# Pooled attention into a mixture of attention experts: a written-out order of work replaced by another one

## The chip, the cores and the metric

The kernel runs on one core of one Trainium2 chip. A core has five engines with instruction queues of their own: TensorE (PE in the profile; PEld are its weight loads), VectorE (DVE), ScalarE (ACT), GpSimd (POOL) and SyncE (SP). Each engine works its queue in order and waits on semaphores for the others. Sixteen DMA engines move data; their transfers are issued here by GpSimd and SyncE. The metric is the time of one execution on the device in microseconds (us), as the median of several runs.

## What is computed

Eight batches. First an attention over pooled keys and values, then a mixture of four experts that are causal attentions themselves; the two best experts of each row are mixed by a softmax of their gate logits.

```python
k_p = k.reshape(B, H, Sp, pool, D).mean(axis=3)          # 576 rows pooled by 8 to 72; v alike
attn = softmax(scale * q @ k_p^T)                         # 8 heads, head size 64
x = (attn @ v_p) as (B, 576, 512)
logits = x @ w_gate                                       # 4 experts, the best 2 are kept
for e in range(E):                                        # each with a head size of 64
    a = softmax(causal(scale * (x @ wq[e]) @ (x @ wk[e])^T))
    out += weight[e] * (a @ (x @ wv[e]) @ wo[e])
```

## The kernel before

**Tiling.** The 576 rows of a batch are four chunks of 128 and a tail of 64; the tails of an even batch and the next odd one share a fifth chunk (index 4), which is worked with the odd batch. Heads are taken in pairs, experts in two groups g of two. PSUM is two pools: joint tiles (`jt`, two buffers) for pooling and scores, and small tiles (four buffers) for everything else. A tile comes free when it is copied out, so a step that takes a small tile waits for the copy of the fourth small tile before it, and one that takes a joint tile for the second before it. Inputs have three buffers per tensor, y has eight.

**Steps.** `plan_weights` (L844) and `plan_batch` (L869) define the work as named steps with their dependencies; nothing is issued there. A step `om3.7` is kind `om`, batch 3, number 7. The kinds, with the line that issues their instructions:

- `lh`, `ld`: half an input load, by GpSimd (L243); per batch 0,1 are k, 2,3 are q, 4,5 are v (`lh` for batch 0, issued in `first`, L807). `wi`: a weight load (L282): 0 wq, 1 wk, 2 wv, 3 the gate's, 4 wo; `wc`: its re-ordering copy on DVE (L865). `ln`, `wl`, `ql`, `xl`, `ol`, `yd` issue nothing: they only mark in the list when a transfer is taken as landed.
- `pk`, `pv`: pooling of k and v by matmuls (L290; batch 0's v in halves, L304); `kp`, `vp`: their copies; `kt`, `qm`: transposes of pooled k and of q on PE (L333, L350), `kT`, `qc`: their copies (L340, L356).
- `am`: scores of a head pair, 4 the tail columns (L370); `ae`: their exponentials on ACT (L376, L385); `om`: attention times v for a chunk and half of the heads (L396; 0 to 4 are chunks of the first half, 5 to 9 of the second); `oi`, `on`: reciprocal and normalisation on DVE (L411, L416) into x.
- `xm`, `xc`: transpose of x on PE and its copy (batches 0 to 3; L428, L436). From batch 4 on, `xd` does it by a DMA transpose on SP (L801), as `qd` does for q from batch 5 on and `od` for the experts' outputs of batches 2 to 6. The first of these transposes waits for all input and weight loads.
- `jm`, `jc`: projections to queries and keys and their copy (L461 and L471; 4 is the tail, L478 and L488); `vm`, `vc`: projections to values and logits, and copies (L441, L451, L452).
- `ga`, `gs`, `gt`, `ge`, `gb`, `gr`, `gc`: the gate's steps (DVE, POOL, DVE, ACT, POOL, DVE, POOL).
- `bm`: expert scores (L568; 0 to 4 in parts, 5 to 7 the shared tail chunk); `be`: their exponentials (L608); `bk`: causal masks on GpSimd (L623); `bo`: the experts' sums (L638; 4, in the last batch 8, is the shared tail chunk, L652 and L659); `bi`, `bg`, `bn`: reciprocal, gate factor, normalisation (L676, L680, L695).
- `ot`, `oc`: transposes of the experts' outputs on PE and copies (batches 0, 1, 7; L700, L707); `ym`, `yc`: the product with wo and its copy (L712, L723); `ys`: a store of y (L727), two DMAs for the shared chunk.
- `fo`, `fn`, `fl`, `fm`, `fc`, `fv`: a range check of all sums' reciprocals, which at the end decides whether a general version is to be run (it isn't on these inputs).
- `mz`: zeros in two buffers; `f` and `F` with a number: a filler of two matmuls on dummy data (`filler`, L766), `f` over 128 rows, `F` over 64, written into the unused end of the small tile that many places back (L775, or L779 where that tile is bf16).

**Order.** The order of the work is the string `ORDER` (L34). `emit` (L132) goes through its words and calls each step, so that the words' order is the order of each engine's queue. A last letter chooses the engine of a step that can be on several: `a` ACT, `d` DVE, `p` POOL, `s` SP. The waits are set by the data and the buffers, not by the string.

```python
    for word in ORDER.split():
        if word[0] in "fF" and word[1:].isdigit():
            filler(word[0] == "F", int(word[1:]))
            continue
        e = {"a": "ACT", "d": "DVE", "p": "POOL", "s": "SP"}.get(word[-1])
        ...
        st.fn(e)
```

Of the kernel before, what the change touches and what calls it, by code (L numbers as in the profile page):

```python
# [45 lines left out]
om1.8 bm0.4 oi1.9 wc0.3 on1.9 oi1.8 bm0.1 om1.3 kT2.0d on1.8 oi1.3 on1.3 xc1.2a be0.4 vm1.2
vm0.0 be0.1 vc1.2d vm0.3 qm2.0 vc0.3a om1.4 bm0.2 be0.2 vc0.0d oi1.4 qc2.0d on1.4 qm2.3 vm0.2
xm1.3 om0.9 bm0.0 qc2.3d am2.3 xc1.3d oi0.9 on0.9 vc0.2a be0.0 qm2.2 qc2.2d vm0.1 qm2.1 xm1.4
vm1.3 vc0.1d qc2.1d xc1.4d om1.6 ae2.3 am2.2 am2.0 ae2.2 jm1.4 ga0.0 vc1.3d oi1.6 on1.6 om1.0
om1.5 xm1.1 oi1.0 oi1.5 on1.5 on1.0 jc1.4d ae2.0 ld2.4 ld3.0 ld2.5 ld3.1 ln2.4 ln2.5 pv2.0  # L50
vp2.0a xc1.1a ld3.2 ln3.0 ln3.1 pk3.0 ln3.2 am2.1 qm3.0 vm1.4 kp3.0a vc1.4a kt3.0 kT3.0a qc3.0d
mz0.0 ld4.2 ln4.2 qm4.0 qm4.1 am2.4 jm1.1 ld4.3 bk0.2 gs0.0 bk0.0 ld3.3 bk0.4 gt0.0 qc4.0d
qc4.1d ae2.1 jm1.3 ge0.0 ae2.4 jc1.3a om2.0 xm1.0 xc1.0a jc1.1d oi2.0 on2.0 ln3.3 bm1.5 qm3.3
qm3.2 om2.2 be1.5 jm1.0 jc1.0a qc3.3d qc3.2d oi2.2 on2.2 om2.7 am3.2 ae3.2 bm1.7 be1.7 om2.6
oi2.7 oi2.6 on2.7 om2.5 oi2.5 on2.6 jm1.2 om2.1 bm1.1 jc1.2a be1.1 ld3.4 ld3.5 bk0.1 ld4.0 bk0.3
ld5.4 ld4.1 on2.5 oi2.1 on2.1 vm1.1 om2.8 qm3.1 xm2.0 oi2.8 on2.8 xc2.0d qc3.1d vc1.1a am3.3
ae3.3 ln3.4 ln3.5 pv3.0 xm2.1 xm2.2 om2.3 vp3.0a bm1.2 be1.2 am3.4 xc2.1d xc2.2d oi2.3 on2.3
# [1415 lines left out]
```

## Time and profile before

| what | value |
|---|---|
| median of three runs | 178.33 us (178.19 to 179.7) |
| the profiled execution | 178.99 us, of which 177.3 us are the span of its instructions |
| PE matmuls | 164.0 us busy, 93% of the span, 2551 recorded |
| ACT, DVE, POOL | 131.3, 122.1, 78.7 us busy |
| DMA | 30.65 MB, 173 GB/s in the mean |
| stores | 31 DMAs issued by SP, 9 by GpSimd |

How to read it: a row of a timeline has the start in us from the beginning of the span, the length, engine, line, operation, output<-inputs, and in brackets how long the engine sat idle before and what released it. PE's rows overlap: the length of a matmul's row runs to the end of its drain, and the next one starts before, so PE's pace is read from start to start. A line of the chain of waits has start, length and what the end of the span was then waiting for.

### The profile page before, as it was taken

Reading aid. Unit: us, or ns where it says so; the run is one execution under the profiler, and the core shown is the slowest. Engines: PE = TensorE matmul, PEld = TensorE weight load, DVE = VectorE, ACT = ScalarE, POOL = GpSimd, SP = SyncE. Lnnn points to the kernel's source line nnn. Section 1 sums busy time; section 2 is a strip of 40 time slices with the busy share of each in tenths; the row PEclk is TensorE's granted clock in tenths of the full one; section 3 lists DMA queues with packets and bytes.
Section 4 is the critical chain, followed back from the end, with each engine's and each line's share of the span. In section 5 each row is a group of like instructions: output and inputs, shape, how many; then the busy total and the mean of one; then the engine's idle time right before and its main releaser. Section 6 shows DMA issues by size and latency. Waiting matters only on the chain.

```text
span 177.3 us, 6308 instructions
## 1 busy us (share of the span) xinstructions
PE 164.0 (93%) x2551; PEld 131.5 (74%) x2566; DVE 122.1 (69%) x466; ACT 131.3 (74%) x239; POOL 78.7 (44%) x179
## 2 busy tenths in 40 slices
...
GB/s 23 196 203 202 200 206 199 206 203 112 200 206 206 204 201 173 187 148 193 41 198 248 175 53 83 157 37 226 166 180 216 134 52 147 239 178 224 254 261 178
DMA packets 44368, 30.65 MB, mean 173 GB/s; under 512 B 24113, under 2 KB 40241, under 8 KB 44337
## 3 DMA queue, kind: packets, MB, share of 16 engines
...
## 4 chain that ended last, share of the span: by engine, by line
PE 82%; ACT 4%; issue 4%; DMA 3%; DVE 3%; POOL 1%; POOLq 0%; DVEq 0%
PE p_ps L461 15%; PE v_ps L441 9%; PE jt L290 9%; PE jt L568 7%; PE oa_ps L396 7%; PE jt L370 6%; PE ob_ps L638 5%; PE y_ps L712 5%; PE fill_ps L775 4%; PE qt_ps L350 3%; DMA oT<-osc 3%; PE xt_ps L428 3%; PE obt_ps L652 2%; PE pt_ps L478 2%; PE kt_ps L333 1%
## 5 line engine op out<-in xcount | busy, mean ns | idle before, releaser
L376 ACT ACTIVATE eta<-jt 72x510 bf16<-72x510 f32 x64 | 34.0, 596 | 7.2 <-PE jt L370 7.1
L416 DVE TENSOR_TENSOR xtm<-oa_ps,za 128x256 bf16<-128x256 f32 (+1 forms) x80 | 32.2, 417 | 1.3
L608 ACT ACTIVATE etc<-jt 128x1024 bf16<-128x1024 f32 x24 | 24.4, 1029 | 1.4 <-PE jt L568 1.2
L441 PE MATMUL v_ps<-wvg,xT 128*128 128x260 bf16 x144 | 20.4, 274 | 0.8 <-DVE osc L695 0.7
L396 PE MATMUL oa_ps<-vpa,eta 72*128 72x65 bf16 x320 | 20.6, 194 | 0.1
L608 ACT ACTIVATE etb<-jt 128x1024 bf16<-128x1024 f32 x16 | 16.2, 1025 | 4.6 <-PE jt L568 4.5
L461 PE MATMUL p_ps<-xT,wq_sb 128*128 128x256 bf16 x128 | 19.2, 272 | 0.1
L461 PE MATMUL p_ps<-xT,wk_sb 128*128 128x256 bf16 x128 | 19.2, 273 | 0.0
L411 DVE RECIPROCAL za<-oa_ps 128x4 f32<-128x4 f32 (+1 forms) x80 | 12.9, 173 | 8.8 <-PE oa_ps L396 7.8
L396 PEld LDWEIGHTS <-eta 72*128 72x128 bf16 x320 | 16.0, 98 | 4.0 <-issue 2.0
L712 PE MATMUL y_ps<-wo_sb,oT 128*128 128x512 bf16 x57 | 16.9, 380 | 1.7 <-DMA oT<-osc 1.6
L623 POOL TENSOR_SCALAR_AFFINE_SELECT etc<-etc 128x512 bf16<-128x512 bf16 x24 | 15.3, 641 | 6.3 <-ACT etc L608 4.4
L568 PE MATMUL jt<-qk 64*128 64x64 bf16 (+4 forms) x208 | 16.3, 260 | 0.0
L441 PEld LDWEIGHTS <-xT 128*128 128x128 bf16 x144 | 12.5, 97 | 4.9 <-issue 1.5
L370 PE MATMUL jt<-qT,kpT 64*72 64x255 bf16 (+1 forms) x256 | 15.7, 238 | 0.3 <-ACT eta L376 0.2
L723 ACT COPY y<-y_ps 128x512 f32<-128x512 f32 x20 | 11.3, 593 | 4.7 <-PE y_ps L712 2.6
L290 PEld LDWEIGHTS <-pm 64*72 64x72 bf16 x270 | 14.2, 110 | 0.8
L723 DVE COPY y<-y_ps 128x512 f32<-128x512 f32 x16 | 10.7, 685 | 5.2 <-PE y_ps L712 2.7
L461 PEld LDWEIGHTS <-wk_sb 128*128 128x128 bf16 x128 | 12.5, 98 | 1.5
L695 DVE TENSOR_TENSOR osc<-ob_ps,gzb 128x256 bf16<-128x256 f32 (+1 forms) x36 | 13.2, 381 | 0.3
L243 POOL DMA_DIRECT2D qb<-in_q_dram x16 | 11.1, 696 | 4.9 <-PE oa_ps L396 2.6
L638 PE MATMUL ob_ps<-vau,etb 128*128 128x65 bf16 x128 | 11.9, 194 | 1.1 <-DVE osc L695 0.6
...
## 6 DMA issues: line engine op xcount, KB each, us to landing
...
```

The source lines that it names most:

```text
L290: nc.tensor.matmul(out=jt[0:SK, hh, 0 : HQ * D], lhsT=pm[r, t, :], rhs=kv[r, t], start=(t == 0), stop=(t == TG - 1),)
L370: nc.tensor.matmul(out=out, lhsT=k_of(kpT, h, w), rhs=rhs, start=True, stop=True)
L376: nc.scalar.activation(out=eta[i][:, 2 * n + z, 0:MAIN].rearrange("p (g i w) -> p g i w", i=QB, w=2), in_=jt[0:SK, :, z * QB * MG : (z + 1 ...
L396: nc.tensor.matmul(out=oa_ps[:, h, :], lhsT=eta[i][:, 4 * w + h, o : o + 128], rhs=vpa[iv][:, 4 * w + h, :], start=True, stop=True,)
L416: nc.vector.tensor_tensor(out=xtm[i if c < MID else 1][r, c, :].rearrange("p (f h e) -> p h f e", f=NF, h=H)[:, 4 * w : 4 * w + 4], in0=oa ...
L441: nc.tensor.matmul(out=v_ps[:], lhsT=xT[i][:, c, f, :], rhs=wvg[:, f, :], start=(f == 0), stop=(f == NF - 1),)
L461: nc.tensor.matmul(out=p_ps[:, z].rearrange("p (c t) -> p c t", c=2), lhsT=w_sb[:, f, g, :], rhs=xT[i][:, 2 * w : 2 * w + 2, f, :], start= ...
L568: nc.tensor.matmul(out=jt[:, ee, o : o + z - a], lhsT=qk[ik][r, 1, g, kc * 128 : (kc + 1) * 128], rhs=qk[iq][r, 0, g, a:z], start=True, st ...
L608: nc.scalar.activation(out=dst, in_=src, func=EXP, scale=B_SCALE)
L638: nc.tensor.matmul(out=ob_ps[:, c - cs[0], :], lhsT=(etb if kc else ets)[i][:, e // 2, e % 2, o : o + 128], rhs=vau[iv][:, kc, e, :], star ...
L712: nc.tensor.matmul(out=y_ps[:], lhsT=oTs[g][:, c, :], rhs=wo_sb[:, g, :], start=(g == 0), stop=(g == NP - 1),)
L723: cp(out=y[:], in_=y_ps)
```

## The change

Only the string `ORDER` differs. The new one holds the same steps, each once, in another order, and differs in these counts:

- fillers: 89 words instead of 68; ahead of the first pooling (`pk0.0`) 45 instead of 37;
- the weights wq, wk, the gate's and wv are loaded behind all of batch 1's inputs; before, wq and wk came behind batch 1's q, and wv and the gate's behind batch 2's k;
- stores (`ys`) by GpSimd 12 instead of 8, by SP 24 instead of 28;
- copies by ACT instead of DVE: kp 7 for 5, jc 21 for 20, xc 8 for 6; by DVE instead of ACT: kT 6 for 5, qc 16 for 13, vc 24 for 21, vp 4 for 3, oc 7 for 4; yc is 20 and 16 in both; gate factors (`bg`) by GpSimd 19 for 16;
- ahead of the first projection (`jm`) now stand pv1, all of batch 0's `om` and all of batch 1's `am`; the experts' sums `bo7.0` to `bo7.7` of the last batch now stand ahead of `bo7.8`, where seven of them stood behind it.

The string has one line more, so lines below it have a number higher by one in the changed kernel. The diff, cut to its beginning, its end and the places that the prediction speaks of:

```diff
-lh0.0 ln0.0 lh0.1 lh0.2 ln0.1 ln0.2 lh0.3 ln0.3 lh0.4 lh0.5 ln0.4 f0 f0 f0 f0 f0 f0 f0 f0 f0 f0
-f0 f0 f0 f0 f0 f0 f0 f0 f0 f0 f0 f0 f0 f0 f0 f0 f0 f0 f0 f0 f0 f0 f0 f0 f0 f0 f0 pk0.0 kp0.0d F0
-F0 F0 F0 F0 F0 F0 qm0.1 kt0.0 kT0.0d qm0.0 qc0.0d qc0.1a f2 f2 f2 f2 qm0.3 f3 f3 am0.1 ae0.1
-qc0.3d qm0.2 am0.3 F4 F4 F4 F4 F4 am0.0 qc0.2a pv0.0 ae0.3 ae0.0 vp0.0d ln0.5 ld1.0 ld1.1 ln1.0
-ln1.1 F4 F4 am0.2 pv0.1 om0.2 ae0.2 vp0.1d om0.0 am0.4 om0.7 om0.1 oi0.2 oi0.7 oi0.0 on0.2 oi0.1
-on0.0 ae0.4 on0.1 on0.7 f4 f4 f4 f4 pk1.0 om0.6 om0.3 oi0.6 oi0.3 on0.6 on0.3 ld1.2 ld1.3 wi0.0
-ln1.2 wi0.1 wl0.1 wl0.0 ln1.3 f3 qm1.0 kp1.0a kt1.0 kT1.0d qc1.0a qm1.1 om0.5 om0.8 f1 f1 qm1.3
-qc1.3a qc1.1d oi0.5 oi0.8 on0.5 on0.8 am1.1 xm0.1 xm0.0 xm0.3 ld1.4 ld1.5 ld2.0 ld2.1 wi0.2
-wi0.3 ld2.2 ld2.3 wl0.2 ln2.2 wl0.3 ln1.4 ln1.5 ln2.0 ln2.1 ae1.1 wc0.0 xc0.1d xc0.3d om0.4
-xc0.0a am1.0 F1 F1 am1.3 xm0.2 qm1.2 oi0.4 wc0.1 ae1.0 xc0.2d on0.4 f4 jm0.0 qc1.2a jm0.2 jc0.0d
-jc0.2d jm0.1 jc0.1d ae1.3 am1.2 ae1.2 pv1.0 jm0.3 vp1.0a om1.2 om1.1 om1.7 am1.4 ae1.4 pk2.0
...
-gc1.0 bk1.4 ld5.3 bk1.3 ln6.3 ln7.2 ln7.3 ln6.5 xc3.2a ln5.3 ln7.5 qd5.0 vc3.4d bi1.4 bg1.4d
...
-bg2.2d bi2.3 ga3.0 bg2.3d bn2.2 on4.2 gs3.0 ys0.0s om5.4 oi5.4 bn2.3 ge3.0 bk2.0 bk2.1 ys0.3s
-xd4.0 xl4.0 vm4.0 vc4.0d on5.4 jm4.2 vp6.0a om5.8 bm3.2 be3.4 be3.2 bm3.1 oi5.8 jc4.2d on5.8
...
-on7.9 bk5.1 gc5.0 bk5.4 bi4.2 bg4.2d jc7.2a yd1.3 bm6.2 bm6.0 be6.2 bo4.0 bo4.1 be6.0 bi4.1
-bi4.0 bn4.2 bo5.4 xl7.1 bm6.4 bm6.1 vm7.3 vc7.3a bk5.2 bg4.0d bi5.4 bg4.1p bn4.0 bn4.1 bk5.0
-bg5.4p bk5.3 bk6.0 ys3.1s bn5.4 ym3.2 vm7.0 yc3.2a vc7.0d yd1.4 xd7.2 od4.0 od4.1 xl7.2 ym3.3
-be6.1 vm7.1 vc7.1a be6.4 bk6.1 vm7.2 vm7.4 ge6.0 yc3.3d vc7.4a vc7.2d yd2.0 jm7.4 bo5.0 ym3.4
-jc7.4a ol4.0 ol4.1 bo5.1 bm6.3 bm7.7 ym4.1 yc3.4a bi5.0 bg5.0d ga7.0 bn5.0 bi5.1 bg5.1d gt7.0
-bn5.1 yd2.2 bk6.2 gs7.0 bk6.4 yd2.1 ym4.0 ys3.2s ys3.0s od5.0 gb6.0 ys3.4p yc4.1a yc4.0d jm7.3
-bo5.3 bo5.2 gr6.0 bi5.3 be6.3 be7.7 ge7.0 jc7.3a bg5.3p jm7.0 bm7.5 bm7.2 bi5.2 bg5.2d jc7.0a
-bn5.3 bn5.2 jm7.1 jc7.1d ym4.2 yd2.3 be7.5 be7.2 yc4.2a ys4.0s bo6.1 ys4.1s bk6.3 gc6.0 gb7.0
-ys3.3s od5.1 bo6.0 bm7.0 bo6.3 be7.0 bo6.2 bi6.1 bg6.1d bi6.0 bn6.1 bi6.3 bg6.0p bn6.0 bi6.2
-bg6.3d bn6.3 bk7.2 bg6.2p bk7.5 bk7.0 gr7.0 bn6.2 ym4.3 bm7.4 be7.4 yd3.0 bm7.1 ol5.1 ol5.0
-yd3.1 yc4.3d ym5.0 yc5.0d be7.1 ym5.3 ym5.2 ym5.4 ym5.1 bm7.6 bm7.3 bk7.4 gc7.0 bk7.1 ys5.0p
-yd3.2 yd3.4 yc5.1a be7.6 yd4.0 ys4.2s od6.0 ol6.0 od6.1 yd3.3 yc5.3d yc5.2d yc5.4d ol6.1 be7.3
-bo7.0 yd5.0 yd4.1 ym6.0 ym6.3 yc6.0a yc6.3a bk7.3 bi7.0 fo7.0 bg7.0d bn7.0 bo7.8 bo7.4 bo7.5
-bi7.8 bi7.4 bg7.8d bi7.5 bn7.8 ym6.1 bg7.4p bo7.3 bn7.4 bg7.5p yd4.2 yc6.1a bn7.5 bo7.2 bo7.1
-bi7.3 bi7.2 bg7.3d bi7.1 bg7.2p bn7.3 bn7.2 bo7.7 bi7.7 bg7.1d bo7.6 ys5.1s ys5.2s ys5.4s bg7.7p
-bi7.6 bn7.1 fn7.0 bg7.6p ys6.3s ys6.1p ys6.0s ys5.3s ys4.3s bn7.7 fl7.0 ot7.1 ot7.0 bn7.6 fm7.0
-fc7.0 yd5.2 oc7.1a oc7.0a ot7.2 ym7.1 yc7.1a yd4.3 yd5.1 yd5.4 yd5.3 yd6.0 ot7.3 ys7.1s ym7.0
-yc7.0a ys7.0s oc7.2d oc7.3d ym7.4 yc7.4a ym7.3 ym7.2 yc7.2a ym6.2 yc7.3a yc6.2d ys6.2p ys7.4s
-ys7.2s ys7.3s yd6.3 yd6.2 yd6.1 yd7.4 yd7.1 yd7.0 yd7.3 yd7.2 fv7.0
+lh0.0 ln0.0 lh0.1 lh0.2 ln0.1 ln0.2 lh0.3 ln0.3 lh0.4 ln0.4 lh0.5 ln0.5 f0 f0 f0 f0 f0 f0 f0 f0
+f0 f0 f0 f0 f0 f0 f0 f0 f0 f0 f0 f0 f0 f0 f0 f0 f0 f0 f0 f0 f0 f0 f0 f0 f0 f0 f0 f0 f0 f0 f0 f0
+f0 f0 f0 f0 f0 pk0.0 F0 F0 F0 F0 F0 F0 F0 qm0.1 qm0.0 qc0.0d kp0.0a kt0.0 kT0.0d qc0.1d f4 f4 f4
+f4 f4 f4 f4 f4 f4 f4 f4 am0.1 ae0.1 qm0.3 qm0.2 am0.0 qc0.3a ae0.0 mz0.0 qc0.2d ld1.0 ld1.1
+ln1.0 ln1.1 ld1.2 ld1.3 ln1.2 ln1.3 ld1.4 ld1.5 wi0.0 wi0.1 wi0.3 wi0.2 F3 pv0.0 am0.2 ae0.2
+vp0.0d F2 F2 F2 F2 F2 om0.0 oi0.0 on0.0 am0.3 F2 F2 F2 am0.4 ae0.3 ae0.4 pv0.1 vp0.1a F2 F2 F2
+F2 F2 F2 F2 om0.7 om0.6 om0.9 om0.5 pk1.0 oi0.9 oi0.7 on0.7 oi0.6 on0.9 on0.6 oi0.5 on0.5 ld2.0
+ld2.1 ld2.2 ld2.3 ld3.0 ld3.2 ld3.3 ld3.1 ld2.4 F4 F4 F4 qm1.0 kp1.0a qm1.1 kt1.0 om0.1 kT1.0d
+qc1.0a qc1.1a wl0.0 wl0.1 f1 f1 f4 qm1.2 oi0.1 on0.1 qc1.2d am1.0 om0.3 om0.8 ae1.0 om0.4 am1.2
+om0.2 oi0.3 oi0.8 on0.3 qm1.3 am1.1 oi0.4 on0.8 xm0.3 oi0.2 qc1.3d on0.4 on0.2 xc0.3d wc0.0
+ln1.4 ln1.5 ae1.2 ae1.1 f2 f2 pv1.0 vp1.0a am1.4 xm0.2 xc0.2d xm0.1 ae1.4 xm0.0 am1.3 om1.4
+om1.2 wl0.3 wl0.2 ln2.0 ln2.1 ln2.2 wc0.1 xc0.1a f1 f1 jm0.1 oi1.2 oi1.4 on1.4 on1.2 jc0.1d
+wc0.3 xc0.0a ae1.3 jm0.0 om1.6 jm0.3 om1.9 jc0.0a bm0.0 bm0.1 om1.7 jc0.3a oi1.6 wc0.2 on1.6
+oi1.9 oi1.7 on1.9 vm0.0 vm0.1 on1.7 vc0.1d vm0.3 jm0.2 vc0.0d be0.0 be0.1 om1.3 om1.0 oi1.3
+vc0.3d oi1.0 on1.0 on1.3 jc0.2a pk2.0 bm0.3 xm1.2 xc1.2d qm2.0 kp2.0a qm2.1 kt2.0 vm1.2 kT2.0a
...
+xc3.2d ae4.2 om3.5 am4.3 am4.1 oi3.5 on3.5 jc2.0a om3.9 ae4.3 ae4.1 bo1.4 bo0.0 xm3.3 bi1.4
+oi3.9 on3.9 bi0.0 bg0.0d xc3.3a bm2.1 be2.1 bk1.4 ld7.2 bg1.4p ld7.1 bk1.0 ld5.3 gs2.0 bk1.3
+gt2.0 ln5.0 ln5.1 pk5.0 kp5.0a ge2.0 bk1.2 bk2.3 ld7.3 bn1.4 bn0.0 ot0.1 xm3.0 xm3.4 xc3.4a
...
+ae4.4 gs3.0 ge3.0 jc3.4a bm3.6 on4.1 bg1.2d bn1.2 oi4.6 gb2.0 gr2.0 on4.6 qd5.0 vp5.0d om4.8
+ot1.0 ql5.0 om4.5 om4.4 am5.4 bk3.1 ys0.0s bk2.4 bk3.4 bk2.1 be3.6 oi4.8 gc2.0 bk2.2 oi4.5 on4.8
...
+on5.8 bg2.2p bn2.2 pk7.0 bm3.2 om5.4 ym1.2 oi5.4 on5.4 bo2.1 xl4.0 vm4.0 ym1.0 kp7.0a ys1.3s
...
+jm7.4 bo4.1 bo4.0 bi4.1 bi4.0 bg4.1p bg4.0d bn4.0 bn4.1 bk5.3 bk5.4 jc7.4a bm6.1 bm6.2 bo4.2
+bi4.2 bg4.2d bn4.2 xl7.1 jm7.3 be6.1 be6.2 jc7.3a jm7.1 bo5.2 bo5.3 bm6.0 bm6.4 bo5.4 xd7.0
+od4.0 ys3.1s od4.1 xl7.0 ys3.2p ys3.0p bi5.2 gc5.0 bg5.2d bi5.3 jc7.1d bk6.2 bk6.1 bk5.0 bn5.2
+bi5.4 bg5.3d bk5.1 bg5.4d bn5.3 bn5.4 jm7.0 jm7.2 be6.4 be6.0 jc7.0d jc7.2a yd2.0 bo5.0 bo5.1
+ym3.4 od5.1 bi5.0 bi5.1 bg5.1d bk6.4 bg5.0p gs6.0 ge6.0 bk6.0 bn5.0 gb6.0 bn5.1 bm7.2 be7.2
+bm7.4 vm7.1 yc3.4d vc7.1d vm7.4 be7.4 yd2.1 ol4.0 ol4.1 vm7.0 vm7.3 vm7.2 vc7.3a vc7.0d gr6.0
+vc7.4d vc7.2a ga7.0 bm6.3 bm7.1 ym4.0 yd3.0 ym4.3 yc4.0d gt7.0 yc4.3d be6.3 ys3.4p bk7.2 gc6.0
+od5.0 ol5.1 ol5.0 ym5.3 ym4.2 bo6.0 bi6.0 yd2.3 yc4.2d ys4.0s ys3.3s yd3.4 yd3.2 gs7.0 bk7.4
+bk6.3 bg6.0p be7.1 bk7.1 bn6.0 ge7.0 yc5.3a bm7.7 be7.7 bm7.0 be7.0 ym5.1 yc5.1a bo6.2 bo6.3
+bo6.1 bi6.2 bi6.3 bg6.2d bi6.1 bg6.1d bg6.3d bn6.2 bn6.3 bn6.1 gb7.0 bk7.5 bk7.0 bm7.3 bm7.6
+ym5.0 ym4.1 yd2.2 yc4.1d gr7.0 be7.3 yd3.1 yc5.0a bk7.3 yd4.0 yd3.3 ym5.4 ym5.2 yc5.4a yc5.2a
+bo7.4 bo7.2 bo7.7 bm7.5 bo7.1 bi7.4 bi7.2 gc7.0 bg7.2p bg7.4d bi7.7 bn7.4 bg7.7p bn7.2 bi7.1
+bo7.0 bg7.1p bn7.7 bi7.0 bo7.6 bg7.0p bi7.6 bn7.1 bo7.3 bo7.5 bi7.3 bn7.0 bg7.6p be7.6 be7.5
+bo7.8 bn7.6 bi7.5 ys5.3s ys4.2s ys4.3s od6.0 od6.1 ys4.1s bg7.3p yd4.1 ol6.1 ol6.0 ym6.0 yc6.0a
+ys5.2s ys5.4s ys5.1p bg7.5p ys5.0p ys6.0s bn7.3 fo7.0 bi7.8 bn7.5 yd4.2 yd4.3 ym6.1 yc6.1a ym6.2
+yc6.2a ys6.1s ys6.2s bg7.8d fn7.0 bn7.8 fl7.0 fm7.0 fc7.0 ot7.2 ot7.3 ym6.3 yd6.0 oc7.3d yd5.0
+yc6.3d yd5.3 yd5.4 ys6.3s yd5.2 yd5.1 ot7.0 oc7.2a ot7.1 ym7.4 yc7.4a ym7.3 oc7.1d oc7.0d ym7.0
+yc7.0d ym7.1 ym7.2 yc7.3a yc7.1a yc7.2d ys7.4s ys7.3s ys7.0s ys7.1s ys7.2p yd6.1 yd6.3 yd7.1
+yd7.0 yd7.4 yd7.2 yd7.3 yd6.2 fv7.0
```

102 lines of the change are left out of this document (48 added, 54 removed).

## The prediction

> **What bounds the kernel now.** I read four views in this order: the page's busy shares, busy time by stage, the chain that ended last, and TensorE's rows in order of time. First the share, then six stages (columns: length, then busy us and instructions of PE, PEld, DVE, ACT, POOL, the granted clock, DMA share, GB/s):
>
> ```profile
> PE 164.0 (93%) x2551; PEld 131.5 (74%) x2566; DVE 122.1 (69%) x466; ACT 131.3 (74%) x239; POOL 78.7 (44%) x179
> ```
> ```profile
> core 0: us, PE busy (x) PEld busy (x) DVE busy (x) ACT busy (x) POOL busy (x), PEclk, DMA share, GB/s
> 0.00:25.40 25.40, 23.09 (x350) 20.72 (x351) 11.58 (x48) 11.80 (x21) 16.39 (x29) 1.00 1.10 170
> 25.40:85.70 60.30, 60.19 (x991) 50.53 (x994) 46.48 (x164) 48.13 (x92) 32.15 (x66) 1.00 1.16 184
> 85.70:153.00 67.30, 65.85 (x1022) 51.31 (x1027) 50.97 (x206) 58.58 (x110) 22.95 (x65) 1.00 0.69 144
> 153.00:162.20 9.20, 7.70 (x98) 4.52 (x100) 6.95 (x21) 6.91 (x10) 4.43 (x12) 1.00 0.95 206
> 162.20:171.00 8.80, 7.21 (x99) 4.38 (x98) 5.51 (x33) 5.25 (x10) 2.21 (x7) 1.00 0.79 274
> 171.00:177.30 6.30, 0.00 (x0) 0.00 (x0) 0.61 (x1) 0.60 (x2) 0.54 (x1) 0.77 0.62 200
> ```
>
> TensorE (PE) is idle 13.3 us in all: 2.3 in the head (1.2 of them before its first instruction), 0.1 and 1.4 in the long middle, 1.5 and 1.6 in the last two working stages, 6.3 in the final stores. So the time is PE's work in its given order, plus few waits, plus the drain. The work itself is the same in both orders, instruction by instruction, except for fillers: dummy matmuls that the order writes in where a wait is expected. What can change is the fillers, the cost of the sequence, and the waits.
>
> **The change part by part.** *Fillers.* The chain of waits (start, length, what) prices them; the third row is the first projection p_ps, step jm0.0:
>
> ```profile
> 1.20 7.13 PE fill_ps L775 x74
> 9.43 0.78 PE fill_ps L775 x14
> 25.40 2.78 PE p_ps L461 x24
> ```
> ```profile
> 11.46 0.61 PE L779 MATMUL kt_ps<-ident,warm 128*128 128x128 bf16 x8 [0.33 <-DVE kpT L340]
> 13.42 0.45 PE L779 MATMUL kt_ps<-ident,warm 64*128 64x64 bf16 x10
> 18.60 0.61 PE L775 MATMUL oa_ps<-warm 128*128 128x128 bf16 x8 [0.52 <-DVE xtm L416]
> ```
>
> A filler word is two matmuls. Seven words took 0.78 us, 0.11 each; the narrow form of 13.42 took about 0.06 a word (starts 0.06 apart, the row's length holds the last one's drain). Ahead of the first pooling (pk0.0) stand 45 words instead of 37: 8 x 0.11 = +0.9 us. Behind it stand 44 instead of 31: three more wide f words, and 19 F words instead of 9, of which 13 instead of 2 are wide by the tile that they write into: 3 x 0.11 + 11 x 0.11 - 1 x 0.06 = +1.5. Together +2.4 us of PE time.
>
> *Weights behind the second batch's inputs.* GpSimd's rows in order of time show that a load is issued when the load eight places earlier has landed:
>
> ```profile
> 18.67 0.75 POOL L282 DMA_DIRECT2D wvs<-in_moe_wv_dram  x1 [0.89 <-DMA qb<-in_q_dram]
> 20.11 0.55 POOL L282 DMA_DIRECT2D wgs<-in_moe_w_gate_dram  x1 [0.69 <-DMA qb<-in_q_dram]
> 21.43 0.69 POOL L243 DMA_DIRECT2D qb<-in_q_dram  x1 [0.77 <-DMA wqs<-in_moe_wq_dram]
> 23.01 0.79 POOL L243 DMA_DIRECT2D qb<-in_q_dram  x1 [0.89 <-DMA wks<-in_moe_wk_dram]
> ```
>
> One load takes about 1.44 us of the stream (18.67 to 20.11). wk landed just before 23.0 as twelfth load; it becomes the fourteenth, behind both halves of batch 1's v: about 25.9, and its re-ordering copy (wc) then takes a fraction of a us. Who waits? The first projection. In the new order 2.3 us more real work stands ahead of it (pv1.0 1.0, am1.2 and am1.4 0.6, om0.9, om1.2, om1.4 0.4, their switches 0.3), and the fillers: 25.4 + 2.3 + 2.4 - 1.0 (next paragraph) = 29.1 us. The later weights are hidden with 3 us to spare; without that cover they would cost up to 2 x 1.44 = 2.9. v of batch 1 comes 2.9 us earlier, which is why pv1.0 can move up.
>
> *Waits in the head.* The rows above show 0.33 and 0.52 us of the 1.1. In the new order eleven f4 words cover the first and seven F2 words the second; following the first batch's exponentials and copies through ACT and DVE, I find short waits at om0.7 and qm1.3, no longer than the drift that the old order has there. Taken: -1.0. Bounds: 0 (fillers come on top) and -1.1 (all idle after 1.2 us gone).
>
> *Sequence.* PE rows around one projection (8 matmuls):
>
> ```profile
> 92.98 0.60 PE L461 MATMUL p_ps<-xT,wq_sb 128*128 128x256 bf16 x4
> 93.42 0.60 PE L461 MATMUL p_ps<-xT,wk_sb 128*128 128x256 bf16 x4
> 93.85 0.29 PE L396 MATMUL oa_ps<-vpa,eta 72*128 72x65 bf16 x4
> 133.49 0.60 PE L461 MATMUL p_ps<-xT,wq_sb 128*128 128x256 bf16 x4
> 134.46 0.61 PE L568 MATMUL jt<-qk 64*128 64x256 bf16 x8
> ```
>
> Start to start 0.87 us where a step of over 64 rows follows, 0.97 where one of 64 rows does (scores, pooling): a switch of the row group costs about 0.1. Counted over both orders there are 118 and 116: -0.2 us.
>
> *The middle.* The same instructions with other neighbours. Eleven copies leave ACT and five come to it, so ACT has some 3 us less, DVE as much more; neither is full between 25.4 and 153 (windows above), so this costs nothing while PE is the cover. One wait of the old order should go, the second of these rows; the step behind it (vm4.0, waiting for a transposed x) has 7 instead of 5.5 us of PE work ahead of it since its last source:
>
> ```profile
> PE y_ps L712 <- DMA oT<-osc: 1.6, 2, 1.3
> PE v_ps L441 <- DVE osc L695: 0.7, 1, 0.7
> ```
>
> Taken -0.7. A new wait of up to 1.5 may replace it somewhere; I bound the middle by -0.7 and +2.
>
> *Stores.* Four more stores on GpSimd (12 for 8) are under 0.6 us each of an engine that is 44% busy, and four fewer on SP, where transposes queue behind stores. Behind them on GpSimd wait masks of scores; the shortest way from a masked score to its reader is 3.3 us of PE work. Nothing; at worst 0.6 at one place.
>
> *The last batch.* Here the order differs most. Prices from the chain and from ACT's groups:
>
> ```profile
> 145.09 1.34 PE v_ps L441 x12
> 147.62 0.43 PE y_ps L712 x2
> 148.05 0.31 PE ob_ps L638 x10
> 148.36 0.44 PE jt L568 x8
> 150.80 0.61 PE ob_ps L638 x20
> 153.32 5.10 DMA oT<-osc
> ```
> ```profile
> L608 ACT ACTIVATE etc<-jt 128x1024 bf16<-128x1024 f32 x24 | 24.4, 1029 | 1.4 <-PE jt L568 1.2
> L723 ACT COPY y<-y_ps 128x512 f32<-128x512 f32 x20 | 11.3, 593 | 4.7 <-PE y_ps L712 2.6 <-PE ob_ps L638 0.9 <-PE jt L568 0.9
> L452 ACT CAST vau<-v_ps 128x256 bf16<-128x256 f32 x15 | 5.9, 396 | 0.0
> ```
>
> My marker is bo7.8, the sum over the last chunk (obt_ps, first row below). Ahead of it the new order puts seven more of the small bo7 sums (+1.1) and two y products fewer (-0.9): +0.2. The 1.6 us that y_ps waited for the transposed oT should mostly go, I take 1.5: od5.1 no longer stands behind stores on SP. But a new wait comes late: bm7.5 and its exponential now stand just ahead of bo7.8. From bm7.2 on ACT has, in order, eight full exponentials (8.2 us), the small be7.7 and ge7.0 (1.0), two v copies with their logits (1.1) and five y copies (3.0): 13.3 us. PE has between bm7.2 and bo7.8 nine y products (3.9), five v (2.2), four bo6 (1.2), eight bo7 sums (1.2), nine score steps (2.0, eight matmuls of two steps being 0.44) and nine switches (0.8): 11.3. With 0.5 from bm7.2 to its exponential bo7.8 waits 13.3 + 0.5 - 11.3 = 2.5 us.
>
> ```profile
> 162.21 0.41 PE L652 MATMUL obt_ps<-vau,ett 128*128 128x65 bf16 x8
> 163.50 0.18 DVE L676 RECIPROCAL zb<-obt_ps 128x4 f32<-128x4 f32 x1 [0.20 <-PE obt_ps L659]
> 164.57 0.41 DVE L695 TENSOR_TENSOR osc<-obt_ps,gzb 128x256 bf16<-128x256 f32 x1
> 170.92 0.69 DVE L723 COPY y<-y_ps 128x512 f32<-128x512 f32 x1 [1.80 <-PE y_ps L712]
> 171.91 0.54 POOL L727 DMA_DIRECT2D out_dram<-y  x1 [3.91 <-DVE y L723]
> ```
>
> Sum for bo7.8: 2.4 - 1.0 - 0.2 - 0.7 + 0.2 - 1.5 + 2.5 = +1.7 us. Behind it the old order needs 9.7 us to its last store (162.21 to 171.91), because seven small sums and their chains through DVE come after it. The new one has only this: sum 1.3, DVE chain to the normalised chunk 1.4, range checks and transposes 1.7 (with one y product), DVE's backlog of three copies 1.4, three y products 1.3, last copy 0.8, store 0.3: 8.2. So -1.5. Total +0.2 us on the profiled execution's own 178.99 (span 177.3), which is 0.66 over the median 178.33 of three. Against the median I say 178.5.
>
> [...] The fillers in the head run at half pace first: the 74 of the first chain row took 7.13 us, though the granted clock reads 1.00 for the stage; 37 words at 0.11 would be 4.1. [...]
>
> **The rivals.**
> - *The oT transpose is late again (slower).* Place: od5.0, od5.1 and ym5.3. ym5.3 has 4.8 us of PE work since its last bo5 sum; in the old order that way took 7.3 us (sum ending at 150.80 + 0.3 to 0.6, landing at 153.32 + 5.10). Then ym5.3 waits 2.4 us, its y copy is in the middle of the full ACT queue, and all of it reaches the end: 178.5 + 2.4 = 180.9. It decides once the way takes over 6 us. For it: y_ps lost 1.6 us to this in the old order. Against: fewer stores ahead on SP.
> - *The first transpose is late (slower).* SP waits for the last input load:
> ```profile
> SPq L801 <- DMA vb<-in_v_dram: 83.2, 1, 83.2
> ```
>   ld7.1 and ld7.3 now stand on GpSimd behind bg1.4, which waits for bo1.4. By bo1.4's place in PE's work they land near 86 us, as the last load did before, and the scores that read the first transpose (am5.4) come some 2 us after it lands. Each us beyond these 2 costs one: 180.5 for a stream that is 4 us late.
> - *The end gives more (faster).* If the y copies reach ACT early enough that bo7.8 does not wait, the 2.5 goes: 176.0. Against: the sums above; for: the lower ACT load before.
> - *The half-pace stretch has another length.* The old 37 words took 7.13 us where full pace is 4.1, so the 45 lie between 5.0 (none at half pace) and 9.9 us, against the 8.0 taken: -3.0 to +1.9. Half the gain gives 177.0. Against: the 7.13 us row, and the first load, which must have landed too. [...]
>
> **How the numbers follow.** About one per cent, 1.8 us, is what I count as a difference. Forecast of no change 45 in 100, with a range of its own from 176.6 to 180.1; oT late 18, first transpose late or another new wait in the middle 17, the end faster 17, half-pace stretch 3 (no change as well). Faster 0.17, within 1% 0.48, slower 0.35. The range goes from 176.0 (the end gives more) to 181.2 (oT late, and 0.3 in the middle).
>
> **What would show it.** Head: pk0.0 near 9.1, first projection near 29 with no wait for wc. Middle: PE idle under 2 us between 30 and 150. End: obt_ps of the last batch released by ACT's ett or etd near 163.9, last store 8.2 us later. The forecast is wrong if y_ps or jt waits for a DMA over 1 us, if the DMA queue of SP is released by loads after 88 us, or if PE's idle in the middle exceeds 3 us.

## The result, and the profile after

The new order takes 181.44 us in the median of 15 runs (179.64 to 184.14), the old one 178.77 us beside it (178.14 to 180.75). The ratio is 1.0106, 95% interval 1.0071 to 1.0142: 1.9 us slower. All ratios leave out runs more than 1.5% above the fastest of their kernel; five of the new order's 15 (183.06 to 184.14) are among them, and none of these five was profiled.

The profiled execution of the new order has a span of 180.0 us, 2.7 more than the old one's 177.3. First its line of busy shares, then the six stages that the prediction showed (same columns; the last stage is longer).

```profile
PE 166.9 (93%) x2608; PEld 132.9 (74%) x2608; DVE 123.9 (69%) x472; ACT 129.3 (72%) x230; POOL 80.7 (45%) x186
```
```profile
core 0: us, PE busy (x) PEld busy (x) DVE busy (x) ACT busy (x) POOL busy (x), PEclk, DMA share, GB/s
0.00:25.40 25.40, 23.97 (x379) 21.68 (x379) 11.45 (x48) 11.63 (x21) 15.69 (x29) 1.00 1.10 169
25.40:85.70 60.30, 59.79 (x955) 49.40 (x953) 45.13 (x165) 47.54 (x84) 30.63 (x61) 1.00 1.15 185
85.70:153.00 67.30, 66.76 (x1066) 52.48 (x1064) 53.32 (x202) 56.51 (x104) 25.52 (x72) 1.00 0.71 141
153.00:162.20 9.20, 7.79 (x106) 4.42 (x104) 6.24 (x25) 7.58 (x16) 5.68 (x16) 1.00 0.71 191
162.20:171.00 8.80, 8.23 (x117) 4.88 (x113) 6.61 (x35) 5.43 (x11) 2.68 (x10) 1.00 0.88 227
171.00:180.00 9.00, 0.37 (x2) 0.00 (x0) 1.15 (x2) 0.56 (x1) 0.54 (x1) 0.67 0.66 220
```

TensorE is idle 1.4 us in the head (2.3 before), 1.05 in the two middle stages (1.56 before), 1.4 and 0.6 in the next two (1.5 and 1.6), and then 8.6 us in the last stage, where it was 6.3. So in these two executions most of the loss stands behind TensorE's last matmul. Read from the trace, in order: the first q transpose (qm0.1) starts at 10.86 instead of 10.14 (+0.7); from there to the end of the last matmul it is 160.5 instead of 160.7 us (-0.2); from the last matmul's end (171.37, before 170.88) to the landing of the last store 6.45 instead of 4.55 (+1.9); and 2.1 instead of 1.8 from there to the span's end (+0.3). Sum +2.7.

What fills the end is seen in stretches of two us: the DMA share, last but one column, and GB/s. The old order first, then the new one.

```profile
161.00:163.00 2.00, 1.89 (x38) 1.36 (x35) 1.81 (x7) 2.00 (x4) 0.00 (x0) 1.00 0.81 305
163.00:165.00 2.00, 1.42 (x31) 0.95 (x28) 1.22 (x7) 1.11 (x4) 1.03 (x3) 1.00 0.89 248
...
169.00:171.00 2.00, 1.88 (x9) 0.62 (x7) 0.20 (x2) 1.74 (x4) 0.00 (x0) 1.00 0.68 256
171.00:173.00 2.00, 0.00 (x0) 0.00 (x0) 0.61 (x1) 0.60 (x2) 0.54 (x1) 1.00 0.97 268
173.00:175.00 2.00, 0.00 (x0) 0.00 (x0) 0.00 (x0) 0.00 (x0) 0.00 (x0) 0.85 0.91 345
175.00:177.00 2.00, 0.00 (x0) 0.00 (x0) 0.00 (x0) 0.00 (x0) 0.00 (x0) 0.50 0.06 16
```
```profile
161.00:163.00 2.00, 2.00 (x40) 1.37 (x39) 1.49 (x7) 1.86 (x5) 1.11 (x4) 1.00 0.33 66
163.00:165.00 2.00, 1.69 (x36) 1.28 (x37) 1.88 (x13) 1.56 (x2) 1.43 (x6) 1.00 0.90 70
...
169.00:171.00 2.00, 2.00 (x12) 0.74 (x9) 0.98 (x4) 1.12 (x3) 0.00 (x0) 1.00 0.91 310
171.00:173.00 2.00, 0.37 (x2) 0.00 (x0) 1.15 (x2) 0.56 (x1) 0.54 (x1) 1.00 1.01 340
173.00:175.00 2.00, 0.00 (x0) 0.00 (x0) 0.00 (x0) 0.00 (x0) 0.00 (x0) 0.76 0.85 246
175.00:177.00 2.00, 0.00 (x0) 0.00 (x0) 0.00 (x0) 0.00 (x0) 0.00 (x0) 0.50 0.98 369
```

In the new order little goes out between 161 and 165 (66 and 70 GB/s, where the old order moved 305 and 248; from 163 on the DMA engines are busy to 0.90 all the same, while the second transpose is in flight), and from 169 to 177 they are nearly full (0.85 to 1.01). SP's queue says why. Old order, then new, each followed by how long SP's stores took to issue (min/median/max in ns) and to land from 161 us on:

```profile
156.35 2.74 SPq L801 DMA_TRANSPOSE oT<-osc  x2
161.23 11.29 SPq L727 DMA_DIRECT2D out_dram<-y  x14
```
```profile
L727 SPq DMA_DIRECT2D out_dram<-y x14: 332/422/1777, 161.2 to 172.1; - x14
...
DMA to landing us min/median/max: 2.1/2.4/4.2
```
```profile
161.00 2.51 SPq L802 DMA_TRANSPOSE oT<-osc  x2
163.60 11.62 SPq L728 DMA_DIRECT2D out_dram<-y  x13
```
```profile
L728 SPq DMA_DIRECT2D out_dram<-y x13: 367/737/1618, 163.6 to 174.5; - x13
...
DMA to landing us min/median/max: 2.9/3.6/4.6
```

The old order had its last two transposes (od6.0, od6.1) out at 159.1. In the new one they are issued from 161.0 to 163.5, and everything behind them on SP goes out from 163.6 on in one row: stores need 3.6 instead of 2.4 us to land, and SP is held up at each (737 instead of 422 ns). GpSimd's last store is issued at 172.46, but SP's last only at 174.5. The last y copy ends at 172.15, and 5.67 us pass until the last byte lands; in the old order 3.82.

### The profile page after: what moved, and what is told of

Its sections match the earlier page's. It is cut to its first block, busy times and chain, and to the rows that moved or that the text cites. A ratio compares the mean times of both kernels' runs of the same rounds, so it can differ in the third digit from the quotient of the medians.

```text
span 180.0 us, 6413 instructions
## 1 busy us (share of the span) xinstructions
PE 166.9 (93%) x2608; PEld 132.9 (74%) x2608; DVE 123.9 (69%) x472; ACT 129.3 (72%) x230; POOL 80.7 (45%) x186
## 4 chain that ended last, share of the span: by engine, by line
PE 76%; ACT 6%; DMA 6%; issue 5%; POOL 2%; POOLq 0%; DVE 0%; ACTq 0%; DVEq 0%
PE p_ps L462 15%; PE v_ps L442 8%; PE jt L291 8%; PE oa_ps L397 7%; PE jt L371 7%; PE y_ps L713 5%; PE fill_ps L776 5%; PE jt L569 5%; PE ob_ps L639 4%; DMA xT<-xtm 3%; PE qt_ps L351 3%; DMA oT<-osc 2%; ACT eta L377 2%; PE pt_ps L479 2%; PE xt_ps L429 2%
## 5 line engine op out<-in xcount | busy, mean ns | idle before, releaser
L377 ACT ACTIVATE eta<-jt 72x510 bf16<-72x510 f32 x64 | 33.3, 596 | 6.9 <-PE jt L371 6.8
L681 POOL TENSOR_TENSOR gzb<-zb,G 128x4 f32<-128x4 f32 (+1 forms) x19 | 3.9, 203 | 41.2 <-DVE zb L677 37.7
L412 DVE RECIPROCAL za<-oa_ps 128x4 f32<-128x4 f32 (+1 forms) x80 | 13.3, 176 | 12.7 <-PE oa_ps L397 11.5
L713 PE MATMUL y_ps<-wo_sb,oT 128*128 128x512 bf16 x72 | 19.3, 380 | 1.7 <-DMA oT<-osc 1.6
L397 PE MATMUL oa_ps<-vpa,eta 72*128 72x65 bf16 x320 | 19.6, 195 | 0.2
L397 PEld LDWEIGHTS <-eta 72*128 72x128 bf16 x320 | 15.4, 98 | 5.3 <-issue 2.7
L371 PE MATMUL jt<-qT,kpT 64*72 64x33 bf16 (+1 forms) x256 | 15.7, 238 | 0.1
L569 PE MATMUL jt<-qk 64*128 64x64 bf16 (+4 forms) x208 | 15.5, 260 | 0.0
L472 ACT CAST qk<-p_ps 128x512 bf16<-128x512 f32 x19 | 11.1, 586 | 6.0 <-PE p_ps L462 5.9
L462 PEld LDWEIGHTS <-wq_sb 128*128 128x128 bf16 x128 | 11.2, 97 | 3.4 <-issue 0.8
```

The source lines that it names most:

```text
L371: nc.tensor.matmul(out=out, lhsT=k_of(kpT, h, w), rhs=rhs, start=True, stop=True)
L377: nc.scalar.activation(out=eta[i][:, 2 * n + z, 0:MAIN].rearrange("p (g i w) -> p g i w", i=QB, w=2), in_=jt[0:SK, :, z * QB * MG : (z + 1 ...
L397: nc.tensor.matmul(out=oa_ps[:, h, :], lhsT=eta[i][:, 4 * w + h, o : o + 128], rhs=vpa[iv][:, 4 * w + h, :], start=True, stop=True,)
L412: nc.vector.reciprocal(out=rz, in_=oa_ps[r, :, D : D + 1])
L462: nc.tensor.matmul(out=p_ps[:, z].rearrange("p (c t) -> p c t", c=2), lhsT=w_sb[:, f, g, :], rhs=xT[i][:, 2 * w : 2 * w + 2, f, :], start= ...
L569: nc.tensor.matmul(out=jt[:, ee, o : o + z - a], lhsT=qk[ik][r, 1, g, kc * 128 : (kc + 1) * 128], rhs=qk[iq][r, 0, g, a:z], start=True, st ...
```

## Experiments

Drain theory: the new order is slower because its stores pile up behind the od6 transposes and drain after the work is done. Rival (PE theory): the end follows TensorE, which is later by its fillers and its wait for oT. Edits are in the string `ORDER` unless told; `...` leaves words out. "Copy to landing" is the time from the end of the last y copy to the landing of the last store, in the one profiled execution of each kernel; "matmul to landing" starts at the end of the last matmul instead. The second is the safer measure, since a y copy may itself wait for a store.

**Stores of the last three batches at half width, in both orders.** The right half of these output rows is not written.

```diff
-        at = eng.dma_start(out=dst, in_=y[r])
+        cw = DM if b < 5 else DM // 2
+        at = eng.dma_start(out=dst[:, 0:cw], in_=y[r, 0:cw])
```


> The new order, with the stores of batches 5 to 7 cut to their left half (the right half of these rows of the output stays unwritten). Drain theory: the end of the new order is set by its stores, which come out of SP's queue in one row from 163.6 us on (13 by SP, 3 by GpSimd, some 3.6 MB at about 345 GB/s) and land at 177.8, while the last y copy ends at 172.15. With half the bytes the row is through soon after the last copy: last landing near 175, 2 to 2.5 us less than the new order's 181.4, about 179. PE theory: the end follows TensorE's last product (fillers and the 1.5 us wait for oT), so halving the stores gives no more than 0.5 us here, and the same amount in the old order.

> The old order with the same cut (right half of the rows of batches 5 to 7 unwritten). Drain theory: the old order's SP stores are issued within 0.6 us of the last copy (171.61 to 172.13), so its queue is hardly backed up: at most 1 us less than 178.8. The distance between the two halved kernels falls to 1 us or less (TensorE ends 0.4 us later in the new order). PE theory: both halved kernels gain alike and keep their distance of 1.9 to 2.7 us.

Measured: new order 178.50 us, ratio 0.9985 (0.9947 to 1.0023); old order 177.55, ratio 0.9930 (0.9890 to 0.9971). Copy to landing is 2.56 us in the one and 2.57 in the other. Halving takes 2.2 us from the new order and 1.25 from the old, and their distance falls from 1.06% to 0.55%, about 1.0 us. So by the runs some 0.9 us of the 1.9 are the bytes of the stores, but the four intervals together leave it anywhere between nothing and 2 us. The traces are clearer: with half the bytes the two orders end alike, matmul to landing 3.35 in the new and 3.30 in the old, where it was 6.45 and 4.55. Each kernel also gains more than the 0.5 that the PE theory allowed. The old order too pays 1.25 us for its last stores, more than the 1 that I allowed.

**Two y products into the wait for oT.**

```diff
-... od5.0 ol5.1 ol5.0 ym5.3 ym4.2 bo6.0 ... ym5.0 ym4.1 yd2.2 yc4.1d ...
+... od5.0 ol5.1 ol5.0 ym4.2 ym4.1 ym5.3 bo6.0 ... yc4.2d yd2.2 yc4.1d ... ym5.0 ...
```


> The new order with two y products (ym4.2, ym4.1) and their copies moved ahead of ym5.3, into TensorE's 1.5 us wait for the transposed oT. Both theories: the wait shrinks to about 0.6 us and TensorE ends some 0.9 us sooner. PE theory: the time falls by the same 0.9, to about 180.5. Drain theory: SP's stores still stand in the same places behind the od6 transposes; these come up to 0.9 us sooner, so the gain is between 0 and 0.9.

Measured: 181.08 us, ratio 1.0115 (1.0054 to 1.0175), so no gain. TensorE's rows with a wait in that stage:

```profile
155.49 0.60 PE L713 MATMUL y_ps<-wo_sb,oT 128*128 128x512 bf16 x2 [0.47 <-DMA oT<-osc]
157.25 0.59 PE L713 MATMUL y_ps<-wo_sb,oT 128*128 128x512 bf16 x2 [0.42 <-DVE y L724]
```

The wait shrank from 1.34 to 0.47, as expected, and a wait for a y copy of 0.42 came behind it. From qm0.1 to the last matmul's end it is 160.3 instead of 160.5. So TensorE did not become 0.9 us faster, as both theories had it, and this run does not decide between them. Matmul to landing is 5.87.

**The same, and two stores ahead of the od6 transposes.**

```diff
-... ys5.3s ys4.2s ys4.3s od6.0 od6.1 ys4.1s ... ys5.1p ...
+... ys5.3s ys4.2s ys4.3s ys4.1s ys5.1s od6.0 od6.1 ...
```


> As the one before, and two stores (ys4.1, already on SP, and ys5.1, which GpSimd issued at 164.5 though its y was copied at 160.1) moved on SP ahead of the od6 transposes, where SP's queue stood empty from 159.2 to 161.0 and the DMA engines were mostly idle. Drain theory: two stores of 0.7 us each less in the row at the end: another 0.7 to 1.4 us faster than the one before. PE theory: no change against the one before, within 0.3 us.

Measured: 179.77 us, ratio 1.0052 (1.0014 to 1.0091), 1.1 us less than the one before. Copy to landing is 3.90 us, nearly the old order's (5.09 in the one before), matmul to landing 4.68 instead of 5.87. SP's last rows:

```profile
156.50 4.43 SPq L728 DMA_DIRECT2D out_dram<-y  x6
162.12 3.71 SPq L802 DMA_TRANSPOSE oT<-osc  x2
165.92 7.70 SPq L728 DMA_DIRECT2D out_dram<-y  x12
```

This is what the drain theory asked for: the row at the end is shorter, and only the places of two stores differ (one of them also went from GpSimd to SP). The intervals of single ratios overlap. Taken together, the kernels of the new order with 45 fillers have 1.0106, 1.0115 and (below) 1.0092 without these moves and 1.0052 with them: about 0.9 us, give or take 0.8. Not all of the gain at the end reaches the time: TensorE took 161.3 us from qm0.1 to its last matmul in this execution, 1.0 more than in the one before. Why is not shown. The expectation had the DMA engines mostly idle while SP's queue stood empty; in the new order's trace they are busy to 0.78 from 159.2 to 161.0 us (291 GB/s), and to 0.33 only from 161 to 163.

**The old order's engines for the stores.** Six letters `p` to `s` (ys0.3, 1.2, 3.2, 3.0, 5.1, 7.2), two `s` to `p` (ys6.1, 6.2), places kept.

> The new order with the stores given to the old order's engines (six from GpSimd back to SP, two the other way: 8 by GpSimd instead of 12), all in their places in the string. Drain theory: the same bytes are stored at the same places behind the od6 transposes, and SP and GpSimd share the DMA engines: within 0.5 us of the new order. Rival, that GpSimd's stores as such cost time by their waits: up to 0.6 us faster.

Measured: 180.68 us, ratio 1.0092 (1.0056 to 1.0127). Same as the new order within the intervals, so GpSimd's share as such does not cost. Matmul to landing is 5.83. Copy to landing is only 4.06 here, because the last copy itself waited for a store to land and free one of the eight y buffers:

```profile
173.03 0.69 DVE L724 COPY y<-y_ps 128x512 f32<-128x512 f32 x1 [1.16 <-DMA out_dram<-y]
```

**Sixteen fillers fewer, in both orders.** `f0` 45 to 29 in the new order, 37 to 21 in the old.

> The new order with 16 fillers fewer ahead of the first pooling (29 words instead of 45), nothing else. Filler theory (as in the prediction): the words ahead of the pooling cost 0.09 to 0.11 us each on the path; without them the pooling starts when its second load has landed, near 7.5 instead of 9.0, everything behind it comes 1.0 to 1.4 us sooner, and the time falls by as much, to about 180. Rival: the head is bound by the loads of q behind it (landing near 9.1 and 10.7) or by TensorE then working its first steps at half pace: less than 0.4 us.

> The old order with 16 fillers fewer ahead of the first pooling (21 words instead of 37). Filler theory: the pooling can start no sooner than its second load lands, near 7.5 instead of 8.3, so 0 to 0.8 us faster, about 178.3; the spread between runs gets smaller if it comes from the length of the half-pace stretch. Rival: the first real steps run at half pace in the fillers' place, so no gain, or a loss of up to 0.5.

Measured: new order 179.43 us, ratio 1.0002 (0.9964 to 1.0041), 1.9 us faster than with 45 (twelve runs from 178.00 to 184.81); old order 184.40 us in the median of twelve (177.13 to 185.55). The ratio for the latter, 0.9969 (0.9885 to 1.0054), rests on two of its runs and says nothing. For the one I had expected 1.0 to 1.4 us less, which lies within its interval; for the other between 0.8 less and 0.5 more, which missed. The heads, new order with 29 words, then old order with 21:

```profile
1.20 5.36 PE L776 MATMUL fill_ps<-warm 128*128 128x128 bf16 x58 [1.20 <-DVE warm L809]
6.49 0.30 PE L291 MATMUL jt<-kb,pm 64*72 64x256 bf16 x1
7.60 1.14 PE L291 MATMUL jt<-kb,pm 64*72 64x256 bf16 x17 [0.81 <-DMA kb<-in_k_dram]
8.50 0.94 PE L776 MATMUL fill_ps<-warm 64*128 64x128 bf16 x14
```
```profile
6.20 0.27 PE L290 MATMUL jt<-kb,pm 64*72 64x256 bf16 x1 [0.77 <-DMA kb<-in_k_dram]
7.58 1.47 PE L290 MATMUL jt<-kb,pm 64*72 64x256 bf16 x17 [1.11 <-DMA kb<-in_k_dram]
8.70 1.70 PE L775 MATMUL fill_ps<-warm 64*128 64x128 bf16 x14
```

In the first, the pooling starts when its load allows, and the next fillers run at full pace (14 in 0.94 us). In the second, TensorE waited twice for loads, 0.77 and 1.11 us, and the same 14 fillers take 1.70: it works at half pace there. So in these two executions the fillers that last nearly until the load is there (29 words) leave the pace whole, and those that end at 5.4 (21 words) do not. The second is an execution of 180.07 us, though; what the seven runs at 184.33 or more paid is not shown.

The 1.9 us of the new order are not all the head's. In its profiled execution qm0.1 starts 1.5 us sooner than with 45 words (9.38 for 10.86), TensorE's way from there is as long as before (160.4), and matmul to landing is 4.92 instead of 6.45: another 1.5 us at the end, though no store was moved. The last transpose landed 2.4 us after its issue here (4.0 with 45 words). So the drain is not a fixed price of the store order, and 6.45 is the longest seen.

**The headline part alone, in the old order.**

```diff
-... ld1.2 ld1.3 wi0.0 ln1.2 wi0.1 ... ld1.4 ld1.5 ld2.0 ld2.1 wi0.2 wi0.3 ld2.2 ...
+... ld1.2 ld1.3 ld1.4 ld1.5 wi0.0 wi0.1 wi0.2 wi0.3 ln1.2 ... ld2.0 ld2.1 ld2.2 ...
```


> The old order with the headline part alone: wq, wk, the gate's and wv loaded right behind batch 1's inputs (v of batch 1 moves ahead of wq and wk). Cover theory: wk lands near 25.9 instead of 23.0 while the old order reaches its first projection at 25.4, so that this step waits some 1.0 to 1.5 us for the copy of wk, and the time rises by about 1 us; in the new order the same loads are hidden because 2.3 us more real work and more fillers stand ahead of that step. Rival: hidden here too, no change within 0.4.

Measured: 179.73 us, ratio 1.0037 (1.0004 to 1.0071): 0.7 us slower, between 0.1 and 1.3. TensorE around the first projection, and DVE's copy of wq:

```profile
25.19 0.38 PE L428 MATMUL xt_ps<-ident,xtm 128*128 128x128 bf16 x4 [1.31 <-DVE xT L436]
...
26.00 1.01 PE L461 MATMUL p_ps<-xT,wq_sb 128*128 128x256 bf16 x4
26.80 1.06 PE L461 MATMUL p_ps<-xT,wk_sb 128*128 128x256 bf16 x4
```
```profile
24.38 0.43 DVE L865 COPY wq_sb<-wqs 128x1024 bf16<-128x1024 bf16 x1 [1.91 <-DMA wqs<-in_moe_wq_dram]
```

The wait is there, 1.31 us. It is named after DVE's copy of x, which in the string stands behind wc0.0, the copy of wq, in DVE's queue: the late load of wq (not of wk, as I had expected) holds up the copy and all behind it. In this execution the projections behind it run at half pace (0.8 us and more from four matmuls to the next four, 0.44 in the prediction's rows; the granted clock is 0.83 in the mean from 20 to 30 us), so here the wait is paid twice. In the new order the first projection (28.72) waits for no weight.

**Attempts at a better old order, and the three corrections of the new one together.** Two edits of the old order (a transpose ahead of three stores; four stores ahead in SP's queue), singly and together; then the new order with both edits above and 37 fillers.

```diff
-... bn5.3 bn5.2 ... ys4.0s bo6.1 ys4.1s ... ys3.3s od5.1 ...
+... bn5.3 bn5.2 od5.1 ... ys4.0s bo6.1 ys4.1s ... ys3.3s ...
-... yc5.4d ol6.1 ... ys5.1s ys5.2s ys5.4s ... ys6.3s ys6.1p ys6.0s ys5.3s ys4.3s ...
+... yc5.4d ys4.3s ys5.3s ys5.2s ys5.4s ol6.1 ... ys5.1s ... ys6.3s ys6.1p ys6.0s ...
```


> The old order with one transpose (od5.1) moved on SP ahead of the three stores that stand before it (ys4.0, ys4.1, ys3.3); it waits for its data until 153.3 in either place, so only the stores move, to behind it. Theory: the transpose took 5.1 us to land because three stores of 256 KB and two more by GpSimd were in flight; without the three it lands 1.5 to 2.5 us sooner, and TensorE's wait of 1.3 us at ym5.x goes. The stores go out at 154.5 to 156 instead of 151 to 153, while SP's queue later stands idle until 161, so the row at the end does not get longer: about 1 us faster than the old order. Rival: the time in flight is the transpose's own, or the moved stores lengthen the row at the end: no gain, within 0.4 us.

> The old order with four stores (ys4.3, ys5.3, ys5.2, ys5.4), whose y is copied between 157.9 and 161.4, moved up on SP from behind ys5.1, ys6.3 and ys6.0 to right behind the transpose od6.1. The queue stood idle from 159.1 to 161.2 there. Drain theory: one or two stores of 0.7 us leave the row at the end; the old order's row is backed up by some 1.2 us (what halving its bytes gave), so 0.3 to 1.2 us faster. Rival: the old order's end is TensorE's last products, no change within 0.3.

> Both edits of the old order together. If both theories hold the gains add, since one is TensorE's wait and the other the drain: 1.3 to 2 us faster than the old order, about 177.2. If the one only moves the end to the other's bound, no more than the larger of the two.

> The new order with its three corrections together: two y products moved into TensorE's wait for oT, two stores ahead of the od6 transposes, and 37 filler words ahead of the first pooling as in the old order instead of 45. Sum theory: 1.1 us (the first two, measured) and 0.7 us (eight words at 0.09) less than the new order, that is the old order's time within 0.5 us. Rival: the head is not on the path, then 1.1 us less than the new order alone and 0.9 us slower than the old.

Measured: 1.0033 (0.9987 to 1.0078), median 181.14 over all twelve (178.40 to 265.20, the longest two 188.52 and 265.20, unexplained); 1.0034 (1.0005 to 1.0063), 179.00 us; 1.0038 (0.9990 to 1.0087), median 181.58 over all twelve; 1.0049 (1.0018 to 1.0080), 179.61 us. All four missed, and no kernel that does the whole work beat the old order clear of noise.

The four moved stores did go out from 158.8 on, and copy to landing stayed at 3.75 us: in the old order it is 3.5 to 3.8 in every full-width trace. Emptying the queue earlier does not shorten it, so there it is set, as it seems, by the last batch's own stores. For the moved transpose, the view of the oT transposes between 150 and 160 us and TensorE's rows:

```profile
L801 SPq DMA_TRANSPOSE oT<-osc x4: 1200/1204/1678, 148.8 to 158.0; - x4
...
DMA to landing us min/median/max: 3.3/3.4/3.9
```
```profile
160.10 0.39 PE L712 MATMUL y_ps<-wo_sb,oT 128*128 128x512 bf16 x1 [1.00 <-DMA oT<-osc]
161.40 0.98 PE L712 MATMUL y_ps<-wo_sb,oT 128*128 128x512 bf16 x3 [0.90 <-DMA oT<-osc]
```
```profile
160.00:165.00 5.00, 4.00 (x55) 3.23 (x56) 1.26 (x8) 1.82 (x3) 0.63 (x1) 0.69 0.84 284
```

The transpose landed after 3.5 instead of 5.1 us, as expected, and ym5.x no longer waited. But ym6.0 and ym6.3, next in the string, came to their own transposes (issued at 156.2 and 158.0) too early and waited 1.00 and 0.90; behind that the granted clock was 0.69 in the mean of five us. In this execution (181.26 us) the wait moved and cost more; why the kernel gained nothing by its ratio either is not shown.

The corrected new order is as far from the old as without the filler edit, which is what the expectation's rival named (0.9 us slower than the old); but the 0.7 us of eight words cannot be seen against intervals of 0.6. In its profiled execution TensorE stood 1.17 us at 167.0 for the range check, a wait that the kernel with 45 words and the same moves does not have.

**The end in all profiled executions.** Matmul to landing, the part in which the two orders differ most:

| kernel | us |
|---|---|
| old order, and its five variants with full stores | 4.25 to 4.55 |
| new order; with the old engines for the stores; with two y products moved | 6.45; 5.83; 5.87 |
| new order with 29 filler words, no store moved | 4.92 |
| new order with two stores ahead of od6, 45 and 37 words | 4.68; 4.69 |
| stores at half width, new and old order | 3.35; 3.30 |

So the new order's excess at the end is 1.3 to 1.9 us with its 45 fillers, and it nearly goes when bytes or stores are taken out of the last row. That it is also small with 29 words, the place of the stores does not explain.

## Why the prediction was right and wrong

The number missed by 2.9 us and lies just above the range's upper end of 181.2; "no change within one per cent" is narrowly off at 1.0106, with the bound inside the interval. 0.4 of the 2.9 are the old order itself (178.77 beside it, 178.33 in the three runs that I started from); the change is 1.9 us where the sum had 0.2. What failed is the term for the stores. Step by step:

- *Fillers ahead, +0.9, pk0.0 near 9.1:* 8.97 against 8.26 in the two profiles. Right there, though it counted on a half-pace stretch as long as in the one profile, and the length varies (below): over all profiled kernels pk0.0 starts between 7.84 and 8.97 with 45 words and between 6.83 and 8.26 with 37, in the mean about 1.0 apart. The loss of 1.9 us that went with 16 words agrees in direction, the eight words of the last experiment do not show; the size stays open between 0 and 1 us.
- *Weights hidden, wk at 25.9, first projection near 29.1:* landed at 25.89, projection at 28.72, no wait for wc. Right; without the cover the part costs 0.7 us in the old order.
- *Head waits -1.0:* idle 2.3 to 1.4, -0.9. *Middle -0.7:* idle 1.56 to 1.05, -0.5. Both right in mechanism: the 0.33 and 0.52 of the head and the 0.7 of v_ps no longer stand among TensorE's waits. The switches' -0.2 no run singles out. The first transpose was not late: the rival of a late load did not come.
- *Stores nothing, at worst 0.6:* this is the step that failed. I asked which engine issues a store and who waits behind it there; I did not ask when its bytes can leave. I saw od5.1 leave its place behind stores, and not that the od6 transposes, now issued at 161.0 instead of 156.35, hold up the stores behind them. Right is that 12 instead of 8 on GpSimd do nothing that can be seen. What I put at nothing is that 13 stores of SP start 2.4 us later and still need nearly all of the DMA engines (0.85 to 1.01 busy from 169 to 177 us): +1.9 us in the profile, +1.3 in two others of the same stores, and by the runs about 0.9 both by halving the stores and by moving two of them, each uncertain by about its own size.
- *Last batch, oT wait -1.5:* failed; y_ps still waits 1.6. *ACT wait +2.5:* failed too; bo7.8 waited 0.16 for ett, the exponentials that it sums, at 164.61 instead of 163.9. ACT took as long as reckoned, 13.7 us from its first exponential of this stretch (150.84) to the end of the last (164.56), for 13.3. TensorE did not: from bm7.2 (150.41) to bo7.8 it took 14.2 instead of 11.3, 1.7 of it idle (1.34 for oT) and the rest work that I had priced 1.2 too low. The oT wait is not all of it: with two y products moved that wait was 0.47, and bo7.8 did not wait for ACT either. That the three misses nearly cancel (+1.5, -2.3, +1.2), so that bo7.8 comes only 0.7 after the 163.9 and TensorE ends only 0.5 later than in the old order, is luck.

```profile
PE y_ps L713 <- DMA oT<-osc: 1.6, 2, 1.3
...
PE p_ps L462 <- DMA xT<-xtm: 0.5, 1, 0.5
PE p_ps L462 <- ACT xT L437: 0.4, 1, 0.4
```
```profile
164.61 0.30 PEld L653 LDWEIGHTS <-ett 128*128 128x128 bf16 x8 [0.16 <-ACT ett L609]
164.62 0.41 PE L653 MATMUL obt_ps<-vau,ett 128*128 128x65 bf16 x8
...
172.46 0.54 POOL L728 DMA_DIRECT2D out_dram<-y  x1 [6.54 <-DVE y L724]
```

- *8.2 us from bo7.8 to the last store:* 7.8 to GpSimd's last. Right for that store, and it was not the last: SP's comes 9.9 us after bo7.8. I had taken the end from the old order's chain, which ends with a store of GpSimd.
- *The rival "oT late":* its wait came (1.34 us at ym5.3, over the 1 us that I had named as a sign, but no longer than the old order's longest), its price did not; shortening it gave nothing. That the time lies near this rival's 180.9 is chance.

Not settled: what the remaining 1.0 us between the two orders with halved stores is. The eight fillers would be 0.9, but nothing shows that alone. Nor is it settled why the drain of one and the same store order varies between 4.92 and 6.45.
